# Attention, eight experts and a GLU in one program: weight splitting moved to VectorE, a first expert in float32, index lists from 128 columns of weights

## The chip, the cores and the metric

The kernel runs on one NeuronCore of a Trainium2 chip. The metric is the device time of one execution in microseconds. Before the change three runs took 915.67, 917.99 and 919.75 us (median 917.99). The profile is of one more execution, whose span from the first to the last instruction is 916.5 us.

## What is computed

Three layers follow one another on 2304 tokens (4 batches of 576) of 512 features, in float32:

```python
# 1. attention: 4 batches, 8 heads, head size 64, window 128, a slope per head
scores = where(0 <= i - j < 128, q @ k.T / 8 - slope[h] * (i - j), -1e9)
x = softmax(scores) @ v                      # -> (2304, 512)

# 2. experts: all (token, expert) logits in falling order; a token takes the first
#    expert that still has room (288 of 2304 tokens each)
logits = x @ w_gate                          # (2304, 8)
for e in range(8):
    out[mask_e] = relu(x[mask_e] @ w1[e]) @ w2[e]     # 512 -> 1024 -> 512

# 3. GLU: the weights arrive as float64
g, val = out @ w_gate2, out @ w_val          # 512 -> 1536
result = (g * sigmoid(g) * val) @ w_out      # 1536 -> 512
```

## The kernel before

Every product of the experts and the GLU is made of three float16 products: each operand is kept as a high and a low float16 part, and `layer` (L1030) adds high x high, low x high and high x low in PSUM. So each of the eight experts needs 624 matmuls of 128 x 128 weights and 288 columns (the last expert splits its last 144 into 288 narrower ones): 96 for the hidden layer (`h`), 96 for its output (`o`), 288 for the GLU's two input products (`gv`), 144 for its output (`y`).

The parts have to be made first.

- **GLU weights** (`glu_weights`, 36 chunks of 128 x 512: 24 for `gv`, 12, called `WO`, for `y`). A chunk comes as 512 KB of float64 (`stg`). DVE shifts the upper words (`shift`, L315) and joins bits (`join`, L319), ACT scales the lower words (`lower`), Pool adds the two as integers (`carry`, L323), ACT writes the high part, and the low part comes from DVE in one instruction (L337) or from Pool in two (L288, L340), whichever the planner takes.
- **Expert weights** (`weights`, 8 chunks of 128 x 1024 for each expert, float32). ACT writes the high part (L950); each half of the low part is one DVE instruction (L955) or two Pool instructions (L958, L959).
- **Activations.** X (tokens turned to columns), H and O are split by ACT and DVE from PSUM (`split`). For each of 12 feature blocks ACT makes the silu, DVE the product `z` (L1083), ACT the high part, and DVE or Pool the low part `P` (L1091).

**Routing** (`route`). One expert at a time: a threshold is found digit by digit in six steps, each a comparison on DVE, counts on PE and small DVE instructions. Then DVE numbers the chosen tokens, writes a one-hot array `oc` (128 x 96 x 18, L851), PE makes the expert's token list from it (`listed`, L856: 18 matmuls, each with 96 columns of `oc` as weights; the columns of one tile lie 18 elements apart), DVE writes `idx` (L863), and Pool gathers the tokens (L988). The first expert's routing stands between attention and everything else. Each later one runs beside the expert before it.

**The order** is written by a planner (`Plan`) while the program is built. Each instruction is a task with an engine (or a choice of two), a cost in us and a due time; on each engine the most urgent task goes first, others where they fit. Costs and dues are estimates (`dve`, `act`, `pool`, `U0`, `EXPERT_US`, `ROUTE`, `TA`); what comes out is a fixed order on each engine, in which an instruction waits for its operands and everything behind it waits too. SP issues the loads in its own order; a load into a buffer still in use holds up the loads behind it. The last four loads of the first expert's weights wait for a Pool memset (`hold`) behind the first gathers.

Of the kernel before, what the change touches and what calls it, by code (L numbers as in the profile page):

```python
# [114 lines left out]
# what passes from the end of one instruction to the start of one that waits for it  # L115
# [4 lines left out]
class Plan:  # L120
    """The order of the instructions.

    A task is one instruction, or a few of one kind, on one engine. Tasks are added in an order in
    which they are right one after another, each with the pieces of data that it reads and writes;
    from these follows what it has to wait for. run() hands them out in the order in which a rough
    model of the engines would start them: on each engine the most urgent one (by `due`) goes first,
    and others go before it only where they fit into the time until it can start. A piece is named
    (ring, instance, part ...); of the rings in `rings` only so many instances live at once.
    """
# [6 lines left out]
    def add(self, engine, us, due, fn, r=(), w=(), late=0.0, soft=False):  # L136
        t = {"on": engine if isinstance(engine, dict) else {engine: us}, "due": due, "fn": fn, "late": late, "soft": soft,
# [44 lines left out]
    def run(self, fit, need=None):  # L182
        """Hands out tasks until all of those in `need` are out."""
# [4 lines left out]
        while left:  # L188
# [22 lines left out]
            self.free[e] = s + us  # L211
            for name in t["slots"]:
# [22 lines left out]
def pool(n, ins=1):  # L235
    return 0.05 + n * ins / 960
# [11 lines left out]
def body(ctx, tc, a, out):  # L248
# [50 lines left out]
    def glu_weights(c, due):  # L299
# [910 lines left out]
```

## Time and profile before

| | before |
|---|---|
| median of three runs | 917.99 us |
| span of the profiled execution | 916.5 us |
| PE busy | 843.2 us, 92%, 7474 matmuls |
| DVE busy | 514.3 us, 56%, 1470 instructions |
| ACT busy | 363.9 us, 40%, 826 instructions |
| Pool busy | 365.3 us, 40%, 402 instructions |
| chain that ended last | PE 61%, DVE 12%, issue 9%, Pool 4% |
| mean granted TensorE clock | 0.955 of full speed |

The profile's busy shares are means over stages: attention up to about 138 us, the first expert's routing, the first two experts with the conversion of the GLU weights beside them, then six experts to the end. The stretches, groups and timelines that matter are shown in the section on the rows.

### The profile page before, as it was taken

The page shows a single profiled execution, that of the slowest core. Times are in us where ns is not written, and L with a number is a line of the kernel's source. Part 1 is how long each engine was busy: PE and PEld are TensorE (multiplying, and loading weights), DVE is VectorE, ACT ScalarE, POOL GpSimd, SP SyncE. Part 2 cuts the span into 40 slices and gives each one's busy share as a digit, 9 for nine tenths or more (in the row PEclk, how much of TensorE's full clock was granted, in tenths as well). Part 3 has the DMA queues.
Part 4 walks back from the last instruction along what each step waited for, and adds up shares of the span by engine and source line. Part 5 has one row for each costly group of instructions (what it writes and reads, how often), then busy time and mean ns, then how long its engine had stood idle before and what let it go on. Part 6 is the DMA issues. An engine that isn't in the chain of part 4 may idle for free.

```text
span 916.5 us, 18887 instructions
## 1 busy us (share of the span) xinstructions
PE 843.2 (92%) x7474; PEld 665.7 (73%) x7474; DVE 514.3 (56%) x1470; ACT 363.9 (40%) x826; POOL 365.3 (40%) x402
## 2 busy tenths in 40 slices
PE   7999982497888899999999999999999999999996
PEld 6898872264566677777787777777777888778786
DVE  4788899899979635634553454346434744311220
ACT  5798972344454323422332233223322435212221
POOL 5588853687867502610351044104410557001001
PEclk9999995688989999999899999999999999999999
DMA  8889423555454202300330042004100535000000
GB/s 289 304 303 315 143 82 98 164 183 161 137 168 136 73 1 93 118 28 1 116 95 28 1 137 74 28 1 153 60 26 1 184 99 164 1 1 27 1 1 26
DMA packets 32167, 92.14 MB, mean 101 GB/s; under 512 B 4048, under 2 KB 10576, under 8 KB 31312
## 3 DMA queue, kind: packets, MB, share of 16 engines
q1 hardware_dynamic: 29008, 81.52, 26.6%
q0 software_dynamic: 3072, 9.44, 3.5%
q8 instruction: 58, 0.95, 0.4%
q14 instruction: 29, 0.24, 0.1%
HBM read 81.51 MB, written 9.44 MB: 99 GB/s over the span
## 4 chain that ended last, share of the span: by engine, by line
PE 61%; DVE 12%; issue 9%; POOL 4%; ACT 2%; DMA 1%; POOLq 0%; DVEq 0%; ACTq 0%
PE mm L1030 53%; PE rp L856 3%; DVE cvu L315 2%; DVE cvt L319 2%; DVE cmp L733 1%; PE mm L1121 1%; POOL cvt L323 1%; DVE WO L337 1%; PE rp L748 1%; DVE WE L955 1%; PE mm L1010 1%; DVE GV L337 1%; PE o L587 1%; PE rp L757 1%; DMA xg<-x_dram,idx 1%
## 5 line engine op out<-in xcount | busy, mean ns | idle before, releaser
L1030 PE MATMUL mm<-O,GV 128*128 128x288 f16 x2304 | 307.3, 294 | 2.7 <-DVE O L978 1.5
L1030 PEld LDWEIGHTS <-GV 128*128 128x128 f16 x2304 | 225.7, 100 | 66.8 <-issue 4.3
L1030 PEld LDWEIGHTS <-WE 128*128 128x128 f16 x1536 | 147.9, 99 | 41.5 <-issue 2.9
L1030 PE MATMUL mm<-P,WO 128*128 128x288 f16 (+2 forms) x1296 | 143.6, 273 | 3.4 <-DVE WO L337 1.8
L1030 PEld LDWEIGHTS <-WO 128*128 128x128 f16 x1296 | 116.6, 98 | 28.7 <-DVE WO L337 2.0
L1091 POOL TENSOR_TENSOR P<-z,P 128x288 f16<-128x288 f32 x22 | 17.4, 792 | 228.2 <-PE mm L1030 208.4
L1030 PE MATMUL mm<-X,WE 128*128 128x288 f16 x768 | 105.1, 294 | 1.1 <-DVE X L978 1.1
L1087 ACT ACTIVATE P<-z 128x288 f16<-128x288 f32 x96 | 42.5, 443 | 157.9 <-DVE z L1083 157.7
L1030 PE MATMUL mm<-P,WE 128*128 128x288 f16 x768 | 97.6, 287 | 0.0
L1129 POOL DMA_INDIRECT out_dram<-R,idx x24 | 23.0, 957 | 174.0 <-ACT R L1125 170.6
L1083 DVE SCALAR_TENSOR_TENSOR z<-mm,t 128x288 f32<-128x288 f32 x96 | 43.6, 454 | 82.5 <-PE mm L1030 74.9
L950 ACT ACTIVATE WE<-stw 128x1024 f16<-128x1024 f32 x64 | 66.6, 1055 | 30.6 <-DMA stw<-in_w_dram 27.3
L959 POOL TENSOR_TENSOR WE<-stw,WE 128x512 f16<-128x512 f32 x57 | 75.7, 1327 | 4.7
L958 POOL TENSOR_SCALAR stw<-stw 128x512 f32<-128x512 f32 x57 | 55.7, 977 | 46.9 <-ACT WE L950 34.8
L955 DVE SCALAR_TENSOR_TENSOR WE<-stw,WE 128x512 f16<-128x512 f32 x71 | 62.2, 892 | 17.5 <-ACT WE L950 17.0
L323 POOL TENSOR_TENSOR cvt<-cvt,cvr 128x512 int32<-128x512 int32 x36 | 52.2, 1455 | 31.8 <-DVE cvt L319 13.2
L976 DVE SCALAR_TENSOR_TENSOR P<-mm,P 128x288 f16<-128x288 f32 x64 | 29.0, 454 | 61.3 <-ACT P L971 60.2
L527 PE MATMUL s<-kt,qb 128*128 128x192 f32 (+2 forms) x288 | 58.6, 339 | 4.7 <-DMA kt<-in_kT_dram 4.4
L1077 ACT ACTIVATE t<-mm 128x288 f32<-128x288 f32 x96 | 39.1, 407 | 57.0 <-PE mm L1030 55.9
L541 ACT ACTIVATE pb<-sc,mx 128x192 f32<-128x192 f32 (+2 forms) x144 | 56.6, 431 | 10.3 <-DVE mx L535 10.0
L971 ACT ACTIVATE P<-mm 128x288 f16<-128x288 f32 x64 | 26.2, 410 | 72.2 <-PE mm L1030 71.7
L1091 DVE TENSOR_TENSOR P<-z,P 128x288 f16<-128x288 f32 x74 | 39.7, 537 | 24.5 <-ACT P L1087 23.3
(137 smaller groups left out, 1169.0 us busy)
## 6 DMA issues: line engine op xcount, KB each, us to landing
stw<-in_w_dram SPq DMA_DIRECT2D x64, 512.0 KB, 3.8
stg<-in_glu_dram SPq DMA_DIRECT2D x36, 512.0 KB, 3.9
qb<-in_qB_dram SPq DMA_DIRECT2D x3, 2304.0 KB, 11.6
x_dram<-xr SPq DMA_DIRECT2D x16, 256.0 KB, 3.2
kt<-in_kT_dram SPq DMA_DIRECT2D x3, 1152.0 KB, 7.4
vf<-in_vN_dram SPq DMA_DIRECT2D x8, 256.0 KB, 4.3
vt<-in_vT_dram SPq DMA_DIRECT2D x4, 512.0 KB, 6.4
vf<-in_vN_dram SPq DMA_DIRECT2D x4, 512.0 KB, 5.9
```

Of the source, the lines that this page charges most:

```text
L323: nc.gpsimd.tensor_tensor(v["t"], v["t"], v["r"], op=OP.add)
L527: nc.tensor.matmul(v["s"][:, par, c:], QB[b % 2][:, hp * 9 + i], KT[b % 2][:, hp, (i - 2) * 64 + c:(i + 1) * 64], start=True, stop=True)
L541: nc.scalar.activation(PB[n % NPB][:, par, 64 * par + c:64 * par + W], v["sc"][:, par, c:], AF.Exp, bias=v["mx"][:, par:par + 1], scale=-1.0)
L950: nc.scalar.activation(WE[:, 0, c], v["f"], AF.Copy, scale=sc)
L955: nc.vector.scalar_tensor_tensor(WE[:, 1, c, at], f[:, at], sc, WE[:, 0, c, at], op0=OP.mult, op1=OP.subtract)
L958: nc.gpsimd.tensor_scalar(f[:, at], f[:, at], sc, 1.0, op0=OP.mult, op1=OP.mult)
L959: nc.gpsimd.tensor_sub(WE[:, 1, c, at], f[:, at], WE[:, 0, c, at])
L1030: nc.tensor.matmul(p[:, :at.stop - at.start], w(i, k), x[:, j, k, at], start=(m == 0), stop=(m == 3 * nk - 1))
L1077: nc.scalar.activation(v["t"], T["mm", k, ("gv", f, 0)][:, :CAP], AF.Silu, scale=1.0 / (SO * SG))
L1083: nc.vector.scalar_tensor_tensor(v["z"], T["mm", k, ("gv", f, 1)][:, :CAP], SPR / (SO * SG), v["t"], op0=OP.mult, op1=OP.mult)
L1087: nc.scalar.activation(P()[:, 0, f], v["z"], AF.Copy)
L1091: eng.tensor_sub(P()[:, 1, f], v["z"], P()[:, 0, f])
```

## The change

1. The first expert's weights are loaded as float32 straight into `WE` and used as they are (`layer32`): one float32 matmul where there were three float16 ones, 32 for the hidden layer and 32 for its output. Its X and H stay float32 too (one copy instead of a split).
2. All low parts of weights and of `P`, and the integer addition of the GLU weights, are done on DVE. Pool keeps its part of attention, the gathers, the stores and memsets.
3. `oc` becomes a fixed array of 128 columns whose last 32 are zero; `listed` loads 128 columns of weights.
4. The planner lets Pool tasks and the DVE tasks marked `port=True` not overlap; costs and dues change (`ROUTE`, `TA`, `TN`, the first expert's pace, the stores `YA`).

Comments were taken out too, so line numbers move. The core of the diff:

```diff
-ROUTE = (-5, 40)
-WA, TA = 7, 12
+ROUTE = ((20, 66), (-5, 30))
+WA = 7
+TA, TN = (12, 22), (1.5, 2.5)
...
+    def ported(self, t, engine):
+        return engine == "Pool" or (engine == "DVE" and t["port"])
     def start(self, t, engine):
         s = self.free.get(engine, 0.0)
+        if self.ported(t, engine):
+            s = max(s, self.free.get("port", 0.0))
...
         def carry(e):
-            nc.gpsimd.tensor_tensor(v["t"], v["t"], v["r"], op=OP.add)
+            nc.vector.tensor_add(v["t"], v["t"], v["r"])
         def low(e):
-            t = v["t"].bitcast(F32)
-            if e == "DVE":
-                nc.vector.scalar_tensor_tensor(parts()[1], t, SG, parts()[0], op0=OP.mult, op1=OP.subtract)
-            else:
-                copy_scaled(e, t, t, SG)
-                nc.gpsimd.tensor_sub(parts()[1], t, parts()[0])
+            nc.vector.scalar_tensor_tensor(parts()[1], v["t"].bitcast(F32), SG, parts()[0], op0=OP.mult, op1=OP.subtract)
...
-        add("DVE", dve(512), due, shift, r=[("stg", c)], w=[("cvu", c)])
+        add("DVE", dve(512, 2), due, shift, r=[("stg", c)], w=[("cvu", c)], port=True)
-        add("Pool", 1.23, due, carry, r=[("cvr", c)], w=[("cvt", c)])
+        add("DVE", 0.66, due, carry, r=[("cvr", c)], w=[("cvt", c)], port=True)
-        add({"DVE": dve(512), "Pool": 1.75}, None, due, low,
+        add("DVE", dve(512), due, low, r=[("cvt", c), (*rows, "hi")], w=[(*rows, "lo")], port=True)
...
+    onehots = big.tile([128, 128, NT], F16, name="oc")
+    add("Pool", 0.5, U0 - 60, lambda e: nc.gpsimd.memset(onehots[:, 96:], 0.0), w=[("onehots",)])
...
-                nc.tensor.matmul(v["pi"][:96, :3], v["oc"][:, :, t], v["rh"][:, t, :], start=(t == 0),
+                nc.tensor.matmul(v["pi"][:, :3], onehots[:, :, t], v["rh"][:, t, :], start=(t == 0),
...
-        do("PE", 0.46, listed, w=[("listed",)] if k == 0 else [])
+        do("PE", 1.2, listed, r=[("onehots",)], w=[("listed",)] if k == 0 else [])
...
-    WE = big.tile([128, 2, 8, 1024], F16, name="WE")
+    WE = big.tile([128, 8, 2, 1024], F16, name="WE")
+    WF = WE.rearrange("p c m f -> p c (m f)").bitcast(F32)
...
+                if k == 0:
+                    v["f"] = WF[:, c]
+                    if c > 3:
+                        hold(v["f"][:, :1])
+                else:
+                    v["f"] = wk.tile([128, 1024], F32, name="stw", bufs=RINGS["stw"])
...
-                add({"DVE": dve(512), "Pool": 1.65}, None, when, lambda e, h=h, low=low: low(e, h),
+                add("DVE", dve(512), when, lambda e, h=h, low=low: low(h),
...
+    def layer32(p, w, x, nk, at=slice(0, CAP)):
+        for k in range(nk):
+            nc.tensor.matmul(p[:, :at.stop - at.start], w(0, k), x[:, k, at], start=(k == 0), stop=(k == nk - 1))
...
+            if first:
+                def hidden(e, f=f):
+                    if e == "ACT":
+                        nc.scalar.activation(single(Hh, 8)()[:, f], T["mm", k, ("h", f)][:, :CAP], AF.Relu)
...
-                        eng = nc.vector if e == "DVE" else nc.gpsimd
-                        eng.tensor_sub(P()[:, 1, f], v["z"], P()[:, 0, f])
+                        nc.vector.tensor_sub(P()[:, 1, f], v["z"], P()[:, 0, f])
...
-            route(k + 1, u + ROUTE[0], u + ROUTE[1])
+            route(k + 1, u + ROUTE[k > 0][0], u + ROUTE[k > 0][1])
```

What the planner makes of it is shown at three places. First DVE at the end of the first expert's routing, from the one-hot array (`oc`) to the list (`idx`); L337 and L344 are low parts of GLU weights, `cvu`, `cvt<-stg` and `cvt<-cvt` are shift, join and carry. Before:

```order
L851 TENSOR_TENSOR oc<-k_slot,po 128x1728
L337 SCALAR_TENSOR_TENSOR GV<-cvt,GV 128x512
L861 TENSOR_SCALAR p_3388<-rp 96x3
L862 TENSOR_SCALAR idx_3003<-rp 96x1
L863 TENSOR_TENSOR idx_3003<-p_3388,rp 96x2
```

After:

```order
L856 TENSOR_TENSOR oc<-k_slot,po 128x1728
L324 SCALAR_TENSOR_TENSOR cvt<-stg,cvu 128x512
L332 ISA cvt<-cvt,cvr 128x1024
L320 TENSOR_SCALAR cvu<-stg 128x512
L866 TENSOR_SCALAR p_3343<-rp 96x3
L867 TENSOR_SCALAR idx_2984<-rp 96x1
L868 TENSOR_TENSOR idx_2984<-p_3343,rp 96x2
```

Three conversions stand where one stood while PE makes the list. Second, DVE at the end of the first expert's GLU input products, where the last `z` and the last low part `P` release the output products. Before, the last two blocks (the `z` and `P` rows) and what stands around them:

```order
L337 SCALAR_TENSOR_TENSOR WO<-cvt,WO 128x512
L1083 SCALAR_TENSOR_TENSOR z<-mm,t 128x288
L337 SCALAR_TENSOR_TENSOR WO<-cvt,WO 128x512
L1091 TENSOR_TENSOR P<-z,P 128x288
L315 TENSOR_SCALAR cvu<-stg 128x512
L337 SCALAR_TENSOR_TENSOR WO<-cvt,WO 128x512
L1083 SCALAR_TENSOR_TENSOR z<-mm,t 128x288
L319 SCALAR_TENSOR_TENSOR cvt<-stg,cvu 128x512
L1091 TENSOR_TENSOR P<-z,P 128x288
```

After, the last block:

```order
L344 SCALAR_TENSOR_TENSOR WO<-cvt,WO 128x512
L802 TENSOR_SCALAR eid_2993<-cd 128x1
L1131 SCALAR_TENSOR_TENSOR z<-mm,t 128x288
L807 TENSOR_SCALAR eq<-code,cd 128x18
L808 SCALAR_TENSOR_TENSOR sg<-bst,ts,eq 128x18
L809 SCALAR_TENSOR_TENSOR sg<-bst,ts,eq 128x18
L1138 TENSOR_TENSOR P<-z,P 128x288
```

The `WO` row here is the last of the twelve: all GLU weights are now made before the last `z`, where five `WO` low parts used to come after it. Third, PE at the start of the first expert's products (L748, L754, L763 and L772 are counts of the second expert's routing). Before:

```order
L748 LDWEIGHTS CH
L748 MATMUL rp<-cmp,CH 32x3x63
L1030 LDWEIGHTS WE
L1030 MATMUL mm<-X,WE 128x288
L1030 LDWEIGHTS WE
L1030 MATMUL mm<-X,WE 128x288
```

After:

```order
L763 LDWEIGHTS c_3418
L763 MATMUL rp<-k_sum,c_3418 63x8
L772 LDWEIGHTS k_unit
L772 MATMUL rp<-fu,k_unit 128x8
L1061 MATMUL mm<-X,WE 128x288 x32
L754 LDWEIGHTS CH
L754 MATMUL rp<-cmp,CH 32x3x63
```

The 32 float32 products of the hidden layer stand in one piece, and the next counts behind them.

## Rows read from the trace of the kernel before

**Rows 1.** Busy time by stretch of the span (us): PE, PEld, DVE, ACT, POOL busy (count), clock, DMA, GB/s.

```profile
138.00:173.00 35.00, 10.68 (x136) 9.07 (x137) 31.12 (x82) 11.37 (x17) 15.94 (x14) 0.50 0.42 139
173.00:183.00 10.00, 5.74 (x31) 2.66 (x30) 9.90 (x18) 2.16 (x6) 7.24 (x8) 0.84 0.38 112
183.00:318.00 135.00, 110.52 (x835) 80.44 (x834) 118.45 (x200) 62.63 (x118) 100.59 (x86) 0.91 0.45 146
318.00:917.00 599.00, 590.67 (x4974) 462.88 (x4973) 245.91 (x657) 179.18 (x370) 145.61 (x160) 0.98 0.18 56
```

**Rows 2.** Timeline, 138 to 173 us: start, duration, engine, line, instruction.

```profile
138.62 1.03 DVE L716 TENSOR_TENSOR w<-logits,bst 128x144 f32<-128x144 f32 x1
...
145.90 1.26 POOL L323 TENSOR_TENSOR cvt<-cvt,cvr 128x512 int32<-128x512 int32 x1 [3.20 <-DVE dg L772]
145.95 1.29 DVE L782 SCALAR_TENSOR_TENSOR thr<-tab,ng,dg 128x64 int32<-128x64 int32 x1
...
165.49 1.19 DVE L831 SCALAR_TENSOR_TENSOR sel<-pe,need,se 128x18 f32<-128x18 f32 x1
...
169.12 3.40 PE L856 MATMUL rp<-rh,oc 128*96 128x3 f16 x18 [5.74 <-DVE oc L851]
...
172.74 0.15 DVE L863 TENSOR_TENSOR idx<-p,rp 96x2 int32<-96x2 f32 x1
```

**Rows 3.** By line, whole span: shortest/median/longest in ns, first and last start.

```profile
L782 DVE SCALAR_TENSOR_TENSOR thr<-tab,ng,dg x7: 274/276/1290, 145.9 to 663.8; 128x64 int32<-128x64 int32 x7
...
L315 DVE TENSOR_SCALAR cvu<-stg x36: 407/721/1832, 69.2 to 288.4; 128x512 int32<-128x512 int32 x36
...
L319 DVE SCALAR_TENSOR_TENSOR cvt<-stg,cvu x36: 669/686/1646, 74.1 to 290.7; 128x512 int32<-128x512 int32 x36
...
L1091 DVE TENSOR_TENSOR P<-z,P x74: 445/458/1522, 229.7 to 891.1; 128x288 f16<-128x288 f32 x74
```

**Rows 4.** Timeline of PE around the lists of later experts.

```profile
361.17 3.40 PE L856 MATMUL rp<-rh,oc 128*96 128x3 f16 x18
364.43 7.51 PE L1030 MATMUL mm<-O,GV 128*128 128x288 f16 x60
...
452.68 10.36 PE L1030 MATMUL mm<-O,GV 128*128 128x288 f16 x60
...
539.38 3.40 PE L856 MATMUL rp<-rh,oc 128*96 128x3 f16 x18
542.64 9.18 PE L1030 MATMUL mm<-O,GV 128*128 128x288 f16 x60
...
720.20 7.71 PE L1030 MATMUL mm<-O,GV 128*128 128x288 f16 x48
```

**Rows 5.** PE by stretch behind one list: busy, TensorE clock, DMA.

```profile
542.70:548.00 5.30, 5.30 (x32) 0.68 0.54 172
```

**Rows 6.** Chain of waits at 130.9 us, and PE's timeline at 393 us.

```profile
130.91 0.93 PE o L587 x24
...
393.49 0.26 PE L757 MATMUL rp<-k_sum,c 128*63 128x8 f16 x3
```

**Rows 7.** Groups by shape on DVE, 183 to 318 us (busy, mean ns, idle before).

```profile
L319 DVE SCALAR_TENSOR_TENSOR cvt<-stg,cvu 128x512 int32<-128x512 int32 x25 | 23.7, 948 | 0.3
L315 DVE TENSOR_SCALAR cvu<-stg 128x512 int32<-128x512 int32 x24 | 21.0, 876 | 0.1
```

**Rows 8.** Groups by shape on POOL, 138 to 304 us.

```profile
L323 POOL TENSOR_TENSOR cvt<-cvt,cvr 128x512 int32<-128x512 int32 x33 | 48.4, 1472 | 31.8 <-DVE cvt L319 13.2 <-DVE fu L760 8.6 <-ACT cvr L285 3.8
```

**Rows 9.** Float32 products on PE (two records each), and DVE's custom instruction.

```profile
61.42 1.54 PE L527 MATMUL s<-kt,qb 128*128 128x192 f32 x8
...
L535 DVE CUSTOM_DVE_ANT_0 sc<-s,bias 128x192 f32<-128x192 f32 x112 | 35.4, 349 | 5.1 <-PE s L527 2.9 <-ACT pb L541 2.2
L535 DVE CUSTOM_DVE_ANT_0 sc<-s,bias 128x64 f32<-128x64 f32 x16 | 3.6, 222 | 8.4 <-PE s L527 7.8 <-ACT tf L567 0.3
```

**Rows 10.** PE's timeline, second expert, first output products.

```profile
318.14 6.05 PE L1030 MATMUL mm<-P,WE 128*128 128x288 f16 x48
```

More of the change, by code (lines that the diff above doesn't have):

```diff
@@ L134, in __init__, with add @@
         self.free, self.count = {}, 0
-    def add(self, engine, us, due, fn, r=(), w=(), late=0.0, soft=False):
-        t = {"on": engine if isinstance(engine, dict) else {engine: us}, "due": due, "fn": fn, "late": late, "soft": soft,
+    def add(self, engine, us, due, fn, r=(), w=(), late=0.0, soft=False, port=False):
+        t = {"on": engine if isinstance(engine, dict) else {engine: us}, "due": due, "fn": fn, "late": late, "soft": soft, "port": port,
              "no": self.count, "deps": [], "next": [], "slots": [], "done": None}
@@ L608, in step @@
                 add("ACT", act(cols, True), due(n, 3.0), whole, r=[("t", n)], w=[("tf", vi)])
-                add({"Pool": pool(cols), "DVE": dve(cols, 2)}, None, due(n, 3.2), high2, r=[("tf", vi)], w=[("th", n)])
+                add({"Pool": pool(cols), "DVE": dve(cols, 2)}, None, due(n, 3.2), high2, r=[("tf", vi)], w=[("th", n)], port=True)
                 add("Pool", pool(cols, 2), due(n, 3.4), low2, r=[("tf", vi), ("th", n)], w=[("tl", n)])
@@ L961, in weights @@
+            if k == 0:
+                when = u - WA + (3.9 * c if c < 4 else 15.6 + 3.9 * (c - 4))
+                add("DMA", dma(2 ** 19), when, fetch, r=[("eid", k)] + [("xg", k, x) for x in range(3 if c > 3 else 0)],
+                    w=[("WE", "hi", c)] + [("WE", "lo", c, h) for h in range(2)], late=LATE)
+                continue
             when = u - WA + (2.96 * c if c < 4 else 11.9 + 2.95 * (c - 4))
-            add("DMA", dma(2 ** 19), when, fetch, r=[("eid", k)] + [("xg", k, x) for x in range(3 if c > 3 and not k else 0)], w=[("stw", (k, c))], late=LATE)
+            add("DMA", dma(2 ** 19), when, fetch, r=[("eid", k)], w=[("stw", (k, c))], late=LATE)
@@ L992, in tokens @@
         for c in range(3):
-            add("Pool", 1.03, u - TA, lambda e, c=c: fetch(e, c),
+            add("Pool", 1.03, u - ta, lambda e, c=c: fetch(e, c),
                 r=[("idx", k)] + [("x_dram", b, kt) for b in range(B) for kt in range(5)], w=[("xg", k, c)])
-            add("DMA", 0.55, u - TA, lambda e: None, w=[("xg", k, c)], late=LATE)
+            add("DMA", 0.55, u - ta, lambda e: None, w=[("xg", k, c)], late=LATE)
         for i in range(WARM if k == 0 else 0):
@@ L1036, in expert, with product @@
     def expert(k, u):
-        def product(when, name, w, x, nk, r, at=slice(0, CAP)):
+        def product(when, name, w, x, nk, r, at=slice(0, CAP), by=layer):
             def fn(e):
                 T["mm", k, name] = bank()
-                layer(T["mm", k, name], w, x(), nk, at)
-            add("PE", 3 * nk * pe(at.stop - at.start), when, fn, r=r, w=[("mm", (k, name)), ("in order",)])
+                by(T["mm", k, name], w, x(), nk, at)
+            add("PE", (3 if by is layer else 4) * nk * pe(at.stop - at.start), when, fn, r=r, w=[("mm", (k, name)), ("in order",)])
         def kept(name, shape, dt, ring):
@@ L1053, in expert, with single @@
         Y = kept("Y", [128, 4, CAP], F32, "Y")
+        def single(name, nk):
+            return lambda: name().rearrange("p m k c -> p (m k c)").bitcast(F32)[:, :nk * CAP].rearrange("p (k c) -> p k c", k=nk)
+        first = k == 0
         for f in range(8):
-            product(u, ("h", f), lambda i, kk, f=f: W1[:, i, f // 2, kk, f % 2 * 128:f % 2 * 128 + 128],
-                    lambda: T["X", k], 4, [("WE", "hi", f // 2)] + [("WE", "lo", f // 2, x) for x in range(2)]
-                    + [y for kd in range(4) for y in both("X", k, kd)])
@@ L1058, in expert @@
[L1058 to L1064 removed]
+            at = slice(f % 2 * 128, f % 2 * 128 + 128)
@@ new lines, in expert @@
+            product(u, ("h", f), lambda i, kk, f=f, at=at: WF1[:, f // 2, kk, at] if first else W1[:, i, f // 2, kk, at],
+                    single(lambda: T["X", k], 4) if first else lambda: T["X", k], 4,
+                    [("WE", "hi", f // 2)] + [("WE", "lo", f // 2, x) for x in range(2)]
+                    + [y for kd in range(4) for y in both("X", k, kd)], by=layer32 if first else layer)
+            u += 1.95 if first else 1.48
+            if first:
+                def hidden(e, f=f):
+                    if e == "ACT":
+                        nc.scalar.activation(single(Hh, 8)()[:, f], T["mm", k, ("h", f)][:, :CAP], AF.Relu)
+                    else:
+                        nc.vector.tensor_scalar(single(Hh, 8)()[:, f], T["mm", k, ("h", f)][:, :CAP], 0.0, None, op0=OP.max)
+                add({"ACT": act(CAP, True), "DVE": dve(CAP)}, None, u, hidden, r=[("mm", (k, ("h", f)))], w=both("P", (k, "H"), f))
+            else:
+                split(u, (k, ("h", f)), lambda f=f: T["mm", k, ("h", f)], ("P", (k, "H"), f),
+                      lambda f=f: (Hh()[:, 0, f], Hh()[:, 1, f]), 1.0, relu=True)
@@ L1065, in expert @@
+        for d in range(4):
+            product(u, ("o", d), lambda i, kk, d=d: WF2[:, d, kk, :] if first else W2[:, i, d, kk, :],
+                    single(Hh, 8) if first else Hh, 8,
+                    [("WE", "hi", 4 + d)] + [("WE", "lo", 4 + d, x) for x in range(2)]
+                    + [y for f in range(8) for y in both("P", (k, "H"), f)], by=layer32 if first else layer)
+            u += 3.9 if first else 2.95
             split(u, (k, ("o", d)), lambda d=d: T["mm", k, ("o", d)], ("O", k, d),
-                  lambda d=d: (O()[:, 0, d], O()[:, 1, d]), SO / (SX * SW1 * SW2))
+                  lambda d=d: (O()[:, 0, d], O()[:, 1, d]), SO if first else SO / (SX * SW1 * SW2))
@@ L1134, in store @@
                 scat.append(i)
-            add("PE", 0.44, ready[c] + YA, turn, r=[("Y", k, d, c) for d in range(4)] + [("ident",)], w=[("mm", (k, "r", c))], soft=True)
-            add("ACT", act(512, True), ready[c] + YA, rows, r=[("mm", (k, "r", c))], w=[("R", (k, c))])
-            add("Pool", 1.2, ready[c] + YA, store, r=[("R", (k, c)), ("idx", k)], late=LATE)
+            when = ready[c] + YA * (1 + c)
+            add("PE", 0.44, when, turn, r=[("Y", k, d, c) for d in range(4)] + [("ident",)], w=[("mm", (k, "r", c))], soft=True)
+            add("ACT", act(512, True), when, rows, r=[("mm", (k, "r", c))], w=[("R", (k, c))])
+            add("Pool", 1.2, when, store, r=[("R", (k, c)), ("idx", k)], late=LATE)
     for c in range(24, 36):
```

68 lines of the change are left out of this document (33 added, 35 removed).

## The prediction

> **What bounds the kernel now.** I read the busy time by stretch first [rows 1], then the timelines at the places where PE waits. Behind 318 us PE is busy 590.7 of 599 us: six experts are bound by PE, and there only PE work taken away, or a better clock, shortens the run. From 138 to 183 us PE works 16 of 45 us: the first expert's routing is a chain through DVE, which is busy 31 of 35 us. From 183 to 318 us (two experts) PE idles 24.5 us at a mean clock of 0.91, while DVE is busy 118 of 135 us and Pool 101: the GLU weights' conversion is the bound. Attention (to 138 us) I leave where it is: before 138 us the order of before puts 12 conversion instructions on DVE beside seven on Pool, that of the change 12 on DVE alone; I allow 1.5 us either way.
>
> In these stages DVE instructions run far over their own shortest time. In the first routing the table instruction takes 1.29 us, its shortest run is 0.274, and a Pool addition began 0.05 us before it and ended with it [rows 2, 3]. Ten such instructions stand between 138.6 and 165.5 us, the first and last in the rows, and add 8.0 us over each one's shortest. From 183 to 318 us the join averages 0.948 us against 0.669, the shift 0.876 against 0.407 [rows 3, 7], with Pool's additions of 1.47 us beside them [rows 8]. I read this as the two engines keeping each other out.
>
> **Part 1, routing.** After attention Pool keeps only gathers, stores and memsets. So the 8.0 us go. The first list's 18 matmuls take 3.40 us [rows 2]; now DVE does a join, a carry and a shift in that time (about 1.7 us by the prices below), and the list is ready when they end: another 1.8 us. `idx`, at 172.9 us, comes at about 163.1. From `idx` to the first product is 10.1 us before (183.0). In the new order DVE has 22 instructions, some 8.2 us, between `idx` and its last copy of X; the tokens' gather takes nearly as long. I take 9.5 us: first product at 172.6.
>
> **Part 2, the list on PE.** 96 columns in 3.31 to 3.40 us / 18 = 0.184 us a load, or 1.92 ns a column; it is the same at half clock (169 us) and full clock (361 us) [rows 1, 2, 4], so the fetch of columns 18 elements apart sets it. What 128 such columns cost no row shows. From above: 128 x 1.92 = 245 ns, 4.4 us a list. From below: loads of 128 adjacent columns pass in (0.93 - 0.2) / 23 = 32 ns each beside 73-column products, 0.6 us a list; 63 adjacent columns take about (0.26 - 0.18) / 2 = 40 ns [rows 6] (0.2 and 0.18 us are what one lone product takes). So a load of the full width is at least 2.5 times as fast per column as a narrower one, and 32 ns may be the product's and not the load's. Divided by 2.5, 245 ns becomes 98 ns, 1.8 us a list. I take 70 ns, 1.3 us, nearer to the row that shares the width: this saves 2.0 us from start to next start (3.26, rows 4) wherever PE is the bound. The ends stay 0.6 and 4.4.
>
> The Trainium skill (TensorE: Matmul & The Clock Gate, section on LDWEIGHTS) makes the load proportional to the columns, which by itself would make 128 a third dearer than 96; its section on Fast Weight Load says that 128 columns of a 2-byte type, strided too, load about twice as fast. By the first alone the result is the rival "no wide load" below; by the second a list would be 2.2 us, and the forecast 6 us later. The 32 ns agree with a fast wide load; its strided form no run here shows.
>
> **Part 3, the clock behind the list.** After four of the six lists behind 318 us the clock falls: 60 products that take 7.51 us behind one list take 10.36 and, twice, 9.18 behind others, and 48 take 7.71 instead of 6.0 [rows 4]; in the first 5.3 us behind one of these lists the clock is 0.68 [rows 5]. Together 2.85 + 2 x 1.67 + 1.7 = 7.9 us. What PE did before was 3.4 us of products of 3 columns. With 1.3 us of them I expect no fall. Kept in full, it is +7.9.
>
> **Part 4, the first expert.** On PE 192 float16 products at (7.51 - 0.17) / 60 = 0.122 us (23.5 us) become 64 float32 ones. Four float32 products of 192 columns take 1.54 us, 0.345 each [rows 9]; by columns that is up to 0.52, and I take 0.49: 31.4 us, 7.9 more, and 3 us more at the half clock in which it starts (row 173 to 183 has 0.84 and a PE half idle). On DVE 16 low parts and 12 splits go, on Pool everything. But DVE is handed the rest. From `idx` to the last `P` of the first expert the new order has on DVE 28 shifts, 29 joins, 29 carries, 30 low parts, 12 `z`, 12 `P`, and 54 others, mostly routing. Prices are shortest times, as Pool no longer stands beside them: 0.41, 0.67 and 0.45 [rows 3], a low part as a join, `z` as `P`. The carry is a custom instruction that no row shows: other custom ones go from 222 ns for 64 elements to 349 for 192 [rows 9], about 1 ns each behind 0.16 us, so 0.68 us for 512 words and 1.2 if each of the 1024 half words passes singly. I take 0.68, since 512 words are what it adds. Sum: 11.5 + 19.4 + 19.7 + 20.1 + 5.4 + 5.4 + 17 = 98 us, less 0.07 for some 120 of them (the next one starts before the recorded end): 90 us. Here DVE is in order, and the split of the first output product waits for PE: ready at 9.5 + 15.7 + 3 + 3.9 + 0.5 = 32.6 us behind `idx`, where DVE could be at 27. So some 6 us of waiting: the last `P` at `idx` + 97 = 260. The 24 GLU input products end on PE at about 246, so DVE sets it, not PE's 7.9 us. ACT makes two passes a chunk beside this and is under 60% busy.
>
> All `WO` parts are made by then, while before PE still waited for them within its output products (part of the 24.5 us that it idles [rows 1]). So 144 products (17.6), a list (1.3), tokens' transposes (1.2), rests of routing (0.3) and 2 us at low clock follow: the second expert starts at 283, and 96 products and small ones (14.4) later its output products at 297.4. Before: 318.1 [rows 10]. Gain 20.7. SP's queue: the last four loads of the first expert's weights still wait for the memsets behind the gathers, with the later GLU chunks behind them; eleven chunks are loaded ahead, which lasts DVE to `idx` + 16, so this is covered. If it were not, DVE waits there, us for us.
>
> **Part 5, from 318 us to the end.** 916.5 - 318.1 = 598.4 us, less six lists x 2.0 = 12.0, less 7.9 of clock, less about 0.5 of a wait for tokens (their gather is due ten us earlier): 578. DVE takes over what Pool did there (146 us busy at Pool's pace, about half at DVE's); it was busy 246 of 599 us [rows 1], so this costs nothing; without that cover every late comparison of the routing would stop PE.
>
> Sum: 297.4 + 578 = 875.5 for the span. The median of the runs stands 1.5 us over this span, so **877**.
>
> **Rivals.** (a) *No wide load*: a list takes 4.4 us. Seven lists on PE's path x 3.1, 2.7 at the first one, and the clock falls as before (7.9): 909. For it: the columns lie apart as before. Against: the 32 ns. (b) *Dear carry*: 1.2 us, 29 x 0.52 and some 3 us in the first routing: 895. (c) *Hand-overs in the first two experts*: PE's order there puts counts of routing between products, each a wait for a DVE that is never idle; PE waited 24.5 us there before. If two thirds of the 20.7 us do not come: 890. Against: the order leaves PE ahead of DVE at all of them. (d) *Slower*: the long DVE instructions are not Pool's doing. Then the shift stays at 0.876 and the others 0.28 us over their shortest: 28 x 0.47 + 100 x 0.28 = 41 us more on the DVE that sets the first expert's end, and 8 more in the routing: 926. It decides once some 45 us of the stretch remain. Against it: each stretched row that I looked at overlaps a Pool instruction, and each line also has runs near its shortest. (e) That the planner's port rule does nothing behind attention is part of the forecast: no Pool task is left there that it could hold apart.
>
> **Numbers.** Forecast 0.66, (a) 0.08, (b) 0.08, (c) 0.13, (d) 0.03; 0.02 that small things cancel to no change. The forecast's own spread is 862 (lists of 0.6 us, no wait for O) to 885. The range 862 to 900 takes in (b) and (c) and leaves out (a) and (d). 0.5% (4.6 us) is about what a measurement of this kernel can tell: faster 0.95, same 0.02, slower 0.03.
>
> **What would show it.** Right: the list about 1.3 us and no half clock behind it; joins near 0.67 us throughout; `idx` near 163; the second expert's output products near 297; an expert in the steady part near 85 us. Wrong: a list of over 2.5 us; DVE instructions still stretched with Pool empty; PE waiting for counts (L754, L763, L772) between 173 and 290 us; carries over 1 us.

## The result, and the profile after

| | before | after |
|---|---|---|
| median (four runs each) | 918.52 us | 879.63 us (877.09 to 880.58) |
| ratio | 1 | 0.9581, interval 0.9558 to 0.9604 |
| span of the profiled execution | 916.5 us | 875.3 us (its own time 877.09) |
| PE / DVE / ACT / Pool busy | 92 / 56 / 40 / 40% | 94 / 57 / 41 / 16% |
| matmuls | 7474 | 7410 |
| mean granted TensorE clock | 0.955 | 0.967 |

The forecast was 877.0 in a range of 862 to 900. Line numbers below are those of the changed kernel unless a sentence says otherwise.

The busy time by stretch of the changed kernel (us: PE, PEld, DVE, ACT, POOL busy with counts, clock, DMA share, GB/s), which answers to [rows 1]:

```profile
138.00:163.00 25.00, 10.70 (x141) 7.68 (x142) 23.86 (x83) 4.71 (x8) 1.10 (x1) 0.50 0.46 157
163.00:173.00 10.00, 6.10 (x30) 3.35 (x29) 7.59 (x17) 3.09 (x6) 2.58 (x7) 0.67 0.92 309
173.00:298.00 125.00, 108.01 (x772) 81.49 (x770) 105.68 (x242) 60.75 (x114) 2.89 (x4) 0.92 0.47 148
298.00:876.00 578.00, 569.27 (x4972) 448.77 (x4970) 255.30 (x710) 181.07 (x372) 43.32 (x65) 1.00 0.19 59
```

The routing stretch is ten us shorter and Pool is all but empty in it; its first DVE instruction and the end of its list (`idx`) in the changed kernel:

```profile
136.27 0.29 DVE L721 TENSOR_REDUCE bst<-logits 128x18 f32<-128x144 f32 x1
...
160.80 0.15 DVE L868 TENSOR_TENSOR idx<-p,rp 96x2 int32<-96x2 f32 x1
```

The long stretch to the end is 21 us shorter, at a clock of 1.00 instead of 0.98. The lists and first products on PE in the changed kernel (timeline: start, duration, engine, line, instruction; a float32 product has two records), answering to [rows 4, 10]:

```profile
159.09 1.29 PE L861 MATMUL rp<-rh,oc 128*128 128x3 f16 x18 [3.81 <-DVE oc L856]
...
172.17 17.61 PE L1061 MATMUL mm<-X,WE 128*128 128x288 f32 x64
...
198.43 8.03 PE L1061 MATMUL mm<-P,WE 128*128 128x288 f32 x32
...
256.39 0.34 PE L754 MATMUL rp<-cmp,CH 128*32 128x96 f16 x6 [11.94 <-DVE cmp L739]
...
261.49 2.81 PE L1055 MATMUL mm<-P,WO 128*128 128x288 f16 x11
...
267.43 1.22 PE L861 MATMUL rp<-rh,oc 128*128 128x3 f16 x18
...
283.66 1.65 PE L1055 MATMUL mm<-X,WE 128*128 128x288 f16 x12
...
298.30 1.89 PE L1055 MATMUL mm<-P,WE 128*128 128x288 f16 x14
...
332.27 1.23 PE L861 MATMUL rp<-rh,oc 128*128 128x3 f16 x18
333.36 14.86 PE L1055 MATMUL mm<-O,GV 128*128 128x288 f16 x120
```

A list takes 1.23 us, and the 120 products behind it run at 0.124 us each: full speed. PE's own longest wait is now 11.94 us for a count of the second expert's routing, from 244.4 us on: DVE, in order, makes most of the last GLU weights (`WO`) first. The join, the shift, the carry, the low part `P` and the table by line over the whole span (shortest/median/longest in ns, first and last start), answering to [rows 3]:

```profile
L324 DVE SCALAR_TENSOR_TENSOR cvt<-stg,cvu x36: 669/684/694, 73.3 to 257.6; 128x512 int32<-128x512 int32 x36
L320 DVE TENSOR_SCALAR cvu<-stg x36: 403/419/1237, 67.4 to 257.1; 128x512 int32<-128x512 int32 x36
L332 DVE CUSTOM_DVE_ANT_0 cvt<-cvt,cvr x36: 675/688/1503, 93.1 to 258.3; 128x1024 uint16<-128x1024 uint16 x36
L1138 DVE TENSOR_TENSOR P<-z,P x96: 448/458/460, 211.9 to 850.2; 128x288 f16<-128x288 f32 x96
L788 DVE SCALAR_TENSOR_TENSOR thr<-tab,ng,dg x7: 276/284/285, 141.3 to 616.5; 128x64 int32<-128x64 int32 x7
```

Medians stand at the shortest times; the long ones that are left (1.50 us of a carry at 134.5 us) lie in attention, where Pool still works.

### The profile page after: what moved, and what is told of

The parts are those of the page before. It is cut to its first block, busy times and chain, and to the rows that moved or that the text cites. A ratio compares the mean times of both kernels' runs of the same rounds, so it can differ in the third digit from the quotient of the medians.

```text
span 875.3 us, 18533 instructions
## 1 busy us (share of the span) xinstructions
PE 818.5 (94%) x7410; PEld 650.1 (74%) x7410; DVE 500.9 (57%) x1570; ACT 357.4 (41%) x815; POOL 142.0 (16%) x208
## 4 chain that ended last, share of the span: by engine, by line
PE 75%; issue 9%; DVE 8%; DMA 3%; ACT 2%; POOL 1%; SPq 0%; POOLq 0%; DVEq 0%; ACTq 0%
PE mm L1055 58%; PE mm L1061 3%; PE s L530 3%; PE o L590 2%; PE t L550 2%; DMA xg<-x_dram,idx 1%; PE mm L1168 1%; PE mm L1024 1%; DVE cvt L324 1%; PE rp L754 1%; DVE cvt L332 1%; PE rp L763 1%; PE rp L861 1%; ACT pb L544 1%; DVE tl L565 1%
## 5 line engine op out<-in xcount | busy, mean ns | idle before, releaser
L1055 PE MATMUL mm<-O,GV 128*128 128x288 f16 x2304 | 292.0, 286 | 0.0
L1055 PEld LDWEIGHTS <-WE 128*128 128x128 f16 x1344 | 129.0, 98 | 32.1 <-issue 0.3
L1055 PE MATMUL mm<-X,WE 128*128 128x288 f16 x672 | 88.0, 286 | 0.0
L1055 PE MATMUL mm<-P,WE 128*128 128x288 f16 x672 | 86.1, 286 | 0.0
L1002 POOL DMA_INDIRECT xg<-x_dram,idx x24 | 25.2, 1049 | 331.0 <-issue 119.0
L965 DVE SCALAR_TENSOR_TENSOR WE<-stw,WE 128x512 f16<-128x512 f32 x112 | 73.5, 684 | 7.3 <-ACT WE L961 6.8
L961 ACT ACTIVATE WE<-stw 128x1024 f16<-128x1024 f32 x56 | 58.6, 1055 | 26.7 <-DMA stw<-in_w_dram 26.6
L1155 ACT ACTIVATE Y<-mm 128x288 f32<-128x288 f32 (+2 forms) x36 | 13.8, 384 | 99.6 <-PE mm L1055 99.5
L530 PEld LDWEIGHTS s<-kt,qb 128*128 128x128 f32 x288 | 45.8, 200 | 6.2 <-DMA qb<-in_qB_dram 4.0
L538 DVE CUSTOM_DVE_ANT_0 sc<-s,bias 128x192 f32<-128x192 f32 (+2 forms) x144 | 41.7, 329 | 11.9 <-DMA bias<-in_cst_dram 5.4
```

What stands on the lines that cost most here:

```text
L530: nc.tensor.matmul(v["s"][:, par, c:], QB[b % 2][:, hp * 9 + i], KT[b % 2][:, hp, (i - 2) * 64 + c:(i + 1) * 64], start=True, stop=True)
L538: nc.vector.tensor_tensor_reduce(out=v["sc"][:, par, c:], in0=v["s"][:, par, c:], in1=bias[:, hp, c:], scale=-0.125, scalar=3.0e38, op0=OP ...
L961: nc.scalar.activation(WE[:, c, 0], v["f"], AF.Copy, scale=sc)
L965: nc.vector.scalar_tensor_tensor(WE[:, c, 1, at], f[:, at], sc, WE[:, c, 0, at], op0=OP.mult, op1=OP.subtract)
L1055: nc.tensor.matmul(p[:, :at.stop - at.start], w(i, k), x[:, j, k, at], start=(m == 0), stop=(m == 3 * nk - 1))
```

## The experiments

Each ratio is against the kernel before on the same chip (917.7 to 918.6 us). In the diffs `...` marks what is left out; the text says what it does.

| run | median us | ratio (interval) |
|---|---|---|
| changed kernel | 879.63 | 0.9581 (0.9558 to 0.9604) |
| e1: changed, list of 96 columns | 902.79 | 0.9841 (0.9824 to 0.9858) |
| e2: before, list of 128 columns alone | 909.49 | 0.9916 (0.9883 to 0.9949) |
| e7: e2 and the due times of later experts | 896.03 | 0.9750 (0.9725 to 0.9776) |
| e3: changed, carry on Pool | 897.93 | 0.9781 (0.9758 to 0.9804) |
| e8: changed, useless additions on Pool | 889.50 | 0.9684 (0.9663 to 0.9704) |
| e4: changed, first expert in float16 parts | 890.74 | 0.9711 (0.9691 to 0.9732) |
| e9: changed, six loads behind the gathers | 880.70 | 0.9596 (0.9567 to 0.9625) |
| e10: changed, no port rule in the planner | 879.26 | 0.9571 (0.9558 to 0.9584) |
| e5: changed, first `y` behind the second expert's `h` and `o` | 864.42 | 0.9411 (0.9390 to 0.9431) |

### The list taken out (e1)

```diff
-                nc.tensor.matmul(v["pi"][:, :3], onehots[:, :, t], v["rh"][:, t, :], start=(t == 0),
+                nc.tensor.matmul(v["pi"][:96, :3], onehots[:, :96, t], v["rh"][:, t, :], start=(t == 0),
```

> The changed kernel, with the lists made from 96 columns of weights again (order of every engine unchanged). My theory: a list takes 3.4 us again instead of the 1.2 to 1.3 of the changed kernel, that is 2.1 us more for each of seven lists that stand in PE's path and 1.8 for the first one, and the clock falls behind some lists come back as they were before (7.9 us in all): 16.5 + 7.9 = 24 us more, about 903 us. Rival A, the clock falls had another cause (Pool's work beside PE, which is gone): no half clock behind the lists and about 895 us. Rival B, the lists are hidden beside waits: within 3 us of the changed kernel.

Measured: 902.79 us, 23.2 more, with 24 expected. One list and the nine us behind it, first the timeline and the busy time by stretch of e1, then the stretch behind the same list of the changed kernel:

```profile
514.96 3.28 PE L861 MATMUL rp<-rh,oc 128*96 128x3 f16 x18
518.10 12.12 PE L1055 MATMUL mm<-O,GV 128*128 128x288 f16 x84
```

```profile
516.00:525.00 9.00, 9.00 (x56) 6.98 (x56) 5.77 (x17) 3.00 (x6) 2.93 (x4) 0.81 0.59 178
```

```profile
504.00:513.00 9.00, 9.00 (x76) 7.18 (x74) 6.26 (x21) 3.94 (x8) 2.96 (x4) 1.00 0.62 185
```

The clock falls to 0.81 of full speed over the nine us behind the 3.28 us of 3-column products, after each of the five lists from 337 to 693 us, while Pool has little but the gathers. It doesn't fall behind 1.23 us of them. Only the list differs, so the fall belongs to the list, and rival A is out. But a long list doesn't always bring it: behind the list at 714.9 us in e1 the clock stays at 1.00, as it did behind two of six in the kernel before (361 and 754 us). What keeps it up there no run shows. The distance from list to list is 88.94 us against 85.2 us: 2.05 of list and 1.7 of clock.

### The list alone, and with the due times (e2, e7)

In the kernel before, `oc` becomes the fixed array of 128 columns (e2), whose tail one more memset on Pool clears; otherwise every engine's order stays.

```diff
-                nc.tensor.matmul(v["pi"][:96, :3], v["oc"][:, :, t], v["rh"][:, t, :], start=(t == 0),
+                nc.tensor.matmul(v["pi"][:, :3], onehots[:, :, t], v["rh"][:, t, :], start=(t == 0),
```

> The kernel before with nothing but the 128-column list (order of every engine unchanged but for one memset on Pool). My theory: the six lists behind 318 us give 2.1 us each (12.6), the clock falls behind them vanish (7.9), the first list gives 1.8, and the one at 263 us up to 2.1: 22 to 24 us less, about 895 us. Rival A, the clock falls have another cause: they stay, and it is about 903 us. Rival B, the 1.3 us list is only to be had with DVE's and Pool's new division: over 910 us.

Measured: 909.49 us, 8.2 less than before on the same chip (917.73) instead of 22 to 24: a miss. PE's timeline of e2 behind a list, and its busy time by stretch behind another:

```profile
356.98 1.28 PE L856 MATMUL rp<-rh,oc 128*128 128x3 f16 x18
358.13 7.51 PE L1030 MATMUL mm<-O,GV 128*128 128x288 f16 x60
365.48 0.33 PE L1010 MATMUL mm<-cst,xg 96*128 96x96 f32 x2
368.00 1.86 PE L1010 MATMUL mm<-cst,xg 96*128 96x96 f32 x10 [2.19 <-DMA xg<-x_dram,idx]
```

```profile
534.00:543.00 9.00, 7.50 (x62) 5.89 (x60) 8.72 (x20) 4.32 (x7) 8.05 (x9) 1.00 0.59 183
543.00:561.00 18.00, 17.13 (x129) 13.22 (x130) 8.79 (x12) 6.99 (x12) 9.83 (x10) 0.91 0.27 89
```

The list is short, and the fall right behind it is gone (1.00). But the order lets only 60 products (7.5 us) stand between the list and the transposes of the gathered tokens, and the gather takes about 9.7 us from the list's end. PE comes earlier and waits, 1.1 to 2.4 us behind each of five lists, and after the three longer waits the clock falls (0.91 over 18 us). Before, with the slow clock behind four of the five lists, PE came late enough not to wait there at all; there the transposes follow the 10.36 us of products [rows 4] without a wait:

```profile
462.88 1.16 PE L1010 MATMUL mm<-cst,xg 96*128 96x96 f32 x12
```

So e7 adds the change's due times for the later experts (`ta` and `tn` replace `TA` and 1.5 for the transposes and splits too):

```diff
-        """The expert's tokens, gathered as rows and turned to columns."""
+        ta, tn = (22, 2.5) if k else (TA, 1.5)
...
-            add("Pool", 1.03, u - TA, lambda e, c=c: fetch(e, c),
+            add("Pool", 1.03, u - ta, lambda e, c=c: fetch(e, c),
...
-            route(k + 1, u + ROUTE[0], u + ROUTE[1])
+            route(k + 1, u + ROUTE[0], u + (30 if k else ROUTE[1]))
```

> The kernel before with the 128-column list, as in the run with the list alone (909.5), and with the due times of the change for the later experts' routing and tokens (the list then stands 120 products ahead of the tokens' transposes instead of 60). My theory: with the list alone PE waited 2.2 us for the gathered tokens behind each of the later lists, and the clock fell after three of these waits (18 us at 0.91, 1.6 us each): the earlier list takes both away, 5 x 2.2 + 3 x 1.6 = 16 us, about 894 us. Rival A, Pool's work on low parts holds the gathers up, and the wait stays: above 905. Rival B, only the wait goes: about 898.

Measured: 896.03 us, 13.5 less than e2 (15 by the ratios, as the two ran on different chips), where I had 16 with all five waits as long as the one in the timeline. From the second expert's output products to the end it takes 893.4 - 313.25 = 580.1 us; before it was 598.4, in e2 906.6 - 313.95 = 592.6. 120 products now cover the gather, and PE doesn't wait in front of the transposes, in e7's timeline:

```profile
434.13 14.86 PE L1030 MATMUL mm<-O,GV 128*128 128x288 f16 x120
448.83 0.41 PE L1010 MATMUL mm<-cst,xg 96*128 96x96 f32 x3
```

The list and the due times make one step: alone the list gives under half of it.

### Pool beside DVE (e8, e3)

e8 puts 12 integer additions on a spare buffer on Pool, behind the start of the first routing.

```diff
-            do("DVE", 0.1, lambda: V.memset(csum, 0.0), r=[*logit_keys, ("CH",)])
+            def adds():
+                s = wk.tile([96, DM], F32, name="R", bufs=RINGS["R"]).bitcast(I32)
+                nc.gpsimd.memset(s, 0)
+                V.memset(csum, 0.0)
+                nc.gpsimd.tensor_copy(s[:, :1], csum[:96])
+                for _ in range(12):
+                    nc.gpsimd.tensor_tensor(s, s, s, op=OP.add)
+            do("DVE", 0.1, adds, r=[*logit_keys, ("CH",)])
```

> The changed kernel, with 12 integer additions of 96 x 512 on Pool, on a buffer that nobody else uses, behind the start of the first expert's routing (138 us); every other engine's order is unchanged. It adds work that nothing waits for but the first gathers (Pool is done by about 156 us, the gathers come at 162). My theory, the two engines keep each other out: DVE instructions of the routing beside them are stretched (comparisons of 0.75 and the table's 0.28 us to over 1 us), idx comes 5 to 9 us later than 160.9, and the kernel takes 885 to 888 us. Rival, no contention: DVE's instructions keep their times, idx at 161, within 2 us of the changed kernel.

Measured: 889.50 us, 9.9 more. The timeline of e8 beside the additions, then that of the changed kernel at the first of the same instructions (carry and shift take 0.688 and 0.419 us there, by their medians above):

```profile
139.51 16.44 POOL L887 TENSOR_TENSOR R<-R 96x512 int32<-96x512 int32 x12
139.69 3.09 DVE L739 TENSOR_TENSOR cmp<-bst,cst 128x567 f16<-128x567 f32 x2
...
142.71 1.52 DVE L344 SCALAR_TENSOR_TENSOR GV<-cvt,GV 128x512 f16<-128x512 f32 x1
...
144.26 0.16 DVE L766 TENSOR_SCALAR fu<-rp 63x8 bf16<-63x8 f32 x1
144.34 1.33 DVE L324 SCALAR_TENSOR_TENSOR cvt<-stg,cvu 128x512 int32<-128x512 int32 x1
...
145.78 0.15 DVE L778 TENSOR_SCALAR dg<-mx 128x1 int32<-128x1 f32 x1
...
149.72 1.52 DVE L332 CUSTOM_DVE_ANT_0 cvt<-cvt,cvr 128x1024 uint16<-128x1024 uint16 x1
...
151.24 1.18 DVE L320 TENSOR_SCALAR cvu<-stg 128x512 int32<-128x512 int32 x1
```

```profile
137.91 1.41 DVE L739 TENSOR_TENSOR cmp<-bst,cst 128x567 f16<-128x567 f32 x2
...
139.23 0.69 DVE L344 SCALAR_TENSOR_TENSOR GV<-cvt,GV 128x512 f16<-128x512 f32 x1
...
140.05 0.16 DVE L766 TENSOR_SCALAR fu<-rp 63x8 bf16<-63x8 f32 x1
140.13 0.67 DVE L324 SCALAR_TENSOR_TENSOR cvt<-stg,cvu 128x512 int32<-128x512 int32 x1
```

Beside Pool the comparison, join, low part, carry and shift grow by 0.65 to 0.85 us; small instructions with a single input keep their time, in PSUM (`fu<-rp`) or in SBUF (`dg<-mx`, 0.15 us in both kernels). From the first routing instruction to the end of `idx` it is 33.3 us instead of 24.7, 8.6 more, for work that nothing needs. So the stretch is Pool's doing, and rival (d) of the prediction, its slower one, falls.

The Trainium skill (SBUF — State Buffer, section Who interferes with whom) says that a DVE instruction with two inputs in SBUF, and one in a two-port mode, contends with a GpSimd instruction that reads SBUF, and that one with at most one SBUF input outside these modes doesn't. The rows agree: the comparison, join, carry and low part have two inputs in SBUF, `dg` has one there and `fu` one in PSUM. The shift has one in SBUF and is stretched, so by that rule it runs in a two-port mode; no run here shows that by itself.

e3 gives the 36 carries back to Pool, at the same places of the order.

```diff
-            nc.vector.tensor_add(v["t"], v["t"], v["r"])
+            nc.gpsimd.tensor_tensor(v["t"], v["t"], v["r"], op=OP.add)
```

> The changed kernel, with the 36 integer additions (carry) given from DVE to Pool, at the same places of the order; DVE has 27 instructions of 0.69 us less between 173 and 262 us. My theory, the two engines keep each other out: joins and shifts beside the additions are stretched again (join mean above 0.80 us, shift above 0.6, in 173 to 262 us), an addition on Pool takes over 1.2 us, and a chunk loses about 1.0 us by it where 0.62 is taken away: 24 x 1.0 - 27 x 0.62 = 7 us more, about 887 us (880 to 895). Rival, no contention: DVE's instructions keep their shortest times, DVE is 17 us earlier at the end of the first expert, PE's wait of 12 us for the counts at 244 us goes, the second expert starts near 268 instead of 283.7, and it is about 863 us.

Measured: 897.93 us, 18.3 more, though DVE has 18.6 us less to do between 173 and 285 us; the sign was right, the size (7 us, 880 to 895) too small. DVE's groups by shape in e3, 173 to 285 us (busy, mean ns, idle before it):

```profile
L320 DVE TENSOR_SCALAR cvu<-stg 128x512 int32<-128x512 int32 x27 | 24.2, 896 | 2.8 <-DMA stg<-in_glu_dram 2.6
L324 DVE SCALAR_TENSOR_TENSOR cvt<-stg,cvu 128x512 int32<-128x512 int32 x27 | 19.1, 708 | 0.2
L344 DVE SCALAR_TENSOR_TENSOR GV<-cvt,GV 128x512 f16<-128x512 f32 x16 | 12.0, 750 | 7.5 <-ACT GV L294 7.4
L344 DVE SCALAR_TENSOR_TENSOR WO<-cvt,WO 128x512 f16<-128x512 f32 x12 | 8.3, 692 | 10.6 <-ACT WO L294 10.6
```

Two costs stand here, and I had only one of them. (A third, 4 us, comes before: the first product starts at 176.2 us instead of 172.2, as the first routing has additions on Pool beside it again.) The shift, which often comes right behind the join and so beside the addition, is stretched (27 x 0.48 = 13 us); the join is not (708, expected over 800). And the low part waits 18 us for ACT's high part, where it waits 3 in the changed kernel, because a chain from DVE over Pool and ACT back to DVE now has to pass while DVE keeps its order. The second list comes at 287.4 us instead of 267.4.

### The first expert (e4)

The first expert's weights, X and H are split again, and its weights are loaded through the staging buffer, with the loads due at the pace of the later experts' loads.

```diff
-                if k == 0:
-                    v["f"] = WF[:, c]
-                    if c > 3:
-                        hold(v["f"][:, :1])
-                else:
-                    v["f"] = wk.tile([128, 1024], F32, name="stw", bufs=RINGS["stw"])
+                v["f"] = wk.tile([128, 1024], F32, name="stw", bufs=RINGS["stw"])
+                if k == 0 and c > 3:
+                    hold(v["f"][:, :1])
...
-        for kd in range(4 if k else 0):
+        for kd in range(4):
...
-        first = k == 0
+        first = False
```

> The changed kernel, with the first expert in three float16 products again: weights split (16 low parts on DVE), X and H split; everything else as changed. My theory, DVE sets the end of the first expert: 16 low parts at 0.62 and 8 splits of H at 0.40 come on top of it, 13 us, less nothing for the 11 us that PE saves: the second expert starts near 297 instead of 283.7, about 892 us. Rival, PE's longer float32 products cost as much as DVE gains: within 4 us of the changed kernel. Second rival, PE sets it: about 868 us.

Measured: 890.74 us, 11.1 more (892 expected); the second expert starts at 295.4 us (297 expected). PE's timeline in e4:

```profile
255.59 16.01 PE L1055 MATMUL mm<-P,WO 128*128 128x288 f16 x108
...
283.95 1.28 PE L861 MATMUL rp<-rh,oc 128*128 128x3 f16 x18 [2.15 <-DVE oc L856]
291.75 0.42 PE L1024 MATMUL mm<-cst,xg 96*128 96x96 f32 x1 [6.53 <-DMA xg<-x_dram,idx]
...
295.44 6.08 PE L1055 MATMUL mm<-X,WE 128*128 128x288 f16 x36
```

The size is near what DVE's extra work says, but it came by another path, so the agreement is in part luck. The first product starts at 179.6 us instead of 172.2, 7.4 later, of which 2.4 lie before the first routing. The output products start at 255.6 us, earlier than in the changed kernel. What is late is the second expert's list, 16.5 us, and it stands behind all 144 output products here, so that no products cover its gather, for which PE waits 6.53 and 1.19 us: from 284 to 296 us PE is busy 4.3 us and DVE only 5.2 of 12. So e4 shows that splitting the first expert costs 11 us in the order that the planner then makes, and neither rival holds. That DVE's added work alone is the cause it doesn't show, as the order changed with it.

### Gathers and loads (e9), the planner's rule (e10)

```diff
-                    if c > 3:
+                    if c > 1:
...
-                add("DMA", dma(2 ** 19), when, fetch, r=[("eid", k)] + [("xg", k, x) for x in range(3 if c > 3 else 0)],
+                add("DMA", dma(2 ** 19), when, fetch, r=[("eid", k)] + [("xg", k, x) for x in range(3 if c > 1 else 0)],
```

> The changed kernel, with six instead of four of the first expert's weight loads held back behind its gathers. In the changed kernel the gathers take 6.4 us to land (4.5 before) while the DMA engines are 92% busy, and the first product starts 11.2 us behind idx where I had 9.5. My theory: two loads less ahead of the gathers let them land 1 to 2 us earlier, first product at 170.5 to 171 instead of 172.2; the kernel within 2 us of the changed one, since DVE sets the end of that expert. Rival: the gathers are slow for another cause, and the first product stays at 172 or later.

Measured: 880.70 us, no change that can be told. The first product starts at 171.08, 9.9 us behind `idx` instead of 11.2, about as expected: with two loads less ahead of the gathers the transposes are through at 170.5 instead of 171.6. DVE hides it: PE then waits 12.91 us for the count at which it waited 11.94.

```diff
-        return engine == "Pool" or (engine == "DVE" and t["port"])
+        return False
```

> The changed kernel, with the planner's port rule switched off (it may again put Pool tasks and marked DVE tasks beside each other); the order changes in attention above all, where Pool still splits probabilities and values, and shifts by some places behind it. My theory: behind attention no Pool task is left that the rule holds apart, and in attention PE is busy 28 to 30 of 30 us from 30 to 120 us whichever way: within 3 us of the changed kernel. Rival: the rule keeps DVE and Pool apart in attention and brings its end (the first routing instruction at 136.3 us, 138.3 before) forward by some 2 us and more, in the shorter routing too: 882 to 886 us.

Measured: 879.26 us, no change. The rule is worth nothing here that can be measured: what keeps the engines apart behind attention is that Pool has nothing to do. The routing starts at 138.5 us in e10 and at 136.3 in the changed kernel, but at 137.9 in e1, which has the changed kernel's order.

### A faster version (e5)

The 11.94 us wait says what to move. DVE makes `WO` while PE has nothing to do, and only the first expert's `y` needs it. e5 puts these products behind the second expert's `h` and `o`; `expert` is cut in three parts for that, H has a buffer of its own, and the rings `stw`, `R` and `cvt` have one instance less each, and the due times of the later experts' tokens change too (`TA`).

```diff
-ROUTE = ((20, 66), (-5, 30))
+ROUTE = ((-10, 35), (-5, 30))
...
-TA, TN = (12, 22), (1.5, 2.5)
-GD = (14, 50)
+TA, TN = (12, 14), (1.5, 2.5)
+GD = (14, 85)
...
-        expert(k, u)
+        expert(k, u, "ho")
+        if k == 1:
+            expert(0, u + 10, "y")
+        expert(k, u, "gv")
+        if k:
+            expert(k, u + 23.6 + 35.5, "y")
```

> The changed kernel, with the first expert's output products of the GLU (y, which need all the WO parts) put behind the second expert's hidden and output products; the second expert's routing is due earlier, the WO conversions later, and rings are cut to make room (stw 2, R 2, cvt 3, H in a buffer of its own). My theory: PE's wait of 12 us for a count at 244 us, and the other 4 to 6 us until 261, come from DVE making WO parts that only y needs; with 26 us of other products ahead of y, DVE has 10 to 14 us more before it is waited for, while it must do 11 us of the second expert's low parts sooner: about 869 us (865 to 874). Rival A, DVE is the bound over the whole stretch to 300 us, and the wait only moves ahead of y: 876 to 881. Rival B, the smaller rings cost more than that gives: over 881.

Measured: 864.42 us, 15 less than the changed kernel and just under the range that I gave. Busy time by stretch, of the changed kernel and of e5:

```profile
246.00:262.00 16.00, 1.31 (x15) 0.87 (x15) 15.62 (x40) 6.54 (x12) 0.00 (x0) 0.55 0.27 87
262.00:298.00 36.00, 35.66 (x303) 27.12 (x301) 25.40 (x69) 14.45 (x25) 2.89 (x4) 0.96 0.42 134
```

```profile
246.00:262.00 16.00, 15.81 (x139) 11.64 (x138) 15.66 (x39) 9.79 (x19) 0.00 (x0) 1.00 0.49 147
262.00:298.00 36.00, 33.03 (x284) 25.31 (x282) 32.12 (x67) 16.12 (x30) 0.00 (x0) 1.00 0.41 126
```

PE is busy 48.84 instead of 36.97 us in these 52 us, 12 more, and never leaves full clock, while DVE works 47.8 instead of 41.0: it had room behind 262 us. The 15 us are those of all these edits together; what the due times and rings give or cost by themselves was not measured.

## Why the prediction was right, point by point

- **Part 1, routing.** From the first routing instruction to the end of `idx` it was 24.7 us, 34.6 before; 24.8 was forecast. `idx` came at 160.95 and not 163.1, as attention ended 2 us earlier; its end differs by as much between runs of one order. From `idx` to the first product it was 11.2 and not 9.5: I took the gathers to last as long as before, but they took 6.4 us to land instead of 4.5, beside float32 weights that no longer wait for a staging buffer. Start 172.2, forecast 172.6: the two errors cancel.
- **Part 2, the list.** 1.23 to 1.29 us; 1.3 was taken. The "no wide load" rival (4.4) is out. The 2.2 us that I worked out from the Trainium skill (TensorE: Matmul & The Clock Gate, Fast Weight Load) were too much: 68 ns for 128 columns 18 elements apart against 184 for 96 is 3.6 times as fast per column, not twice. The section's claim that strided columns load fast holds.
- **Part 3, the clock.** No half clock behind a list, and e1, with the long lists, brings the falls back, behind five of the six lists from 337 us on (four of six before).
- **Part 4, the first expert.** 64 float32 products took 33.9 us (31.4 and 3 forecast), 0.50 each at full clock. The carry took 0.688 (0.68 taken), so "dear carry" is out. The last `P` started at 261.3 (260), the second expert at 283.7 (283), its output products at 298.3 (297.4). The time of the last `P` is closer than its working: from `idx` it was 100.4 us and not 97, with DVE's work as forecast (89.2 us, 90) but 11.2 us of waits instead of some 6, and the early `idx` made up for most of it. That DVE and not PE sets this is read from the trace (over 246 to 262 us DVE is busy 15.62 of 16 us, PE 1.31) and borne out by e5, where 15 us go when PE has other products there; e4 shows only what the split costs. Rival (c), hand-overs in the first two experts, was there: the wait of 11.94 us for a count is its kind; but it lies where the DVE sum already had PE waiting, so it took nothing from the gain.
- **Part 5, to the end.** 577.0 us (578). The sum holds, one of its terms does not stand by itself: I gave 12 us to the lists, 7.9 to the clock, and 0.5 to tokens that come earlier. By e2 the first two give 5.8 us without the earlier tokens; e7 adds the other 12.5. I had read the slow stretch as pure cost. It also covered the gather. The changed kernel takes 3.1 us less than e7 here, which was not taken apart.
- **The slower rival.** e8 rules it out: Pool's work stretches DVE, 8.6 us in this routing, where the rows before gave 8.0.
- **(e), the port rule** does nothing behind attention, as said (e10).

Sum: 298.3 + 577.0 = 875.3, forecast 875.5. That it is 0.2 us off is luck: 0.9 too late and 1.0 too early cancel, and this is the shortest of the four executions (875.3 to 878.7). The median, 879.63, stands 4.3 us above this span where I had 1.5.

## What to carry to other kernels

Sum the in-order engine's instructions at their undisturbed times and see whether that, or the engine with the longest busy bar, sets the end; where PE waits for an engine that is never idle, look for products that need less of its work and put them first (15 us here). When a stall or a slow stretch is taken away, ask what it covered: here a gather, which had to be ordered earlier before the gain came. And an instruction given to a second engine has three prices: its own time, what it does to its neighbour, and the hand-overs of the chain that it joins.

## What the runs showed of the hardware that I had not expected

- Pool suffers too: an addition of 96 x 512 takes 1.37 us (median) beside DVE's instructions and 1.04 at the shortest (e8).
- The clock is at its lower level (0.50 of full, 1.2 GHz) through the whole first routing, in which PE is busy 10.7 of 25 us, and falls in the 12 us wait (0.55 over 246 to 262 us). In e5, with PE busy 15.8 of these 16 us, it stays at 1.00.
- A short wait can cost twice: in e2 a wait of 2.2 to 2.4 us was followed, three times of five, by 18 us at a mean clock of 0.91.
